# Strassen's seven products for gate and up in the last token block of a bilinear FFN

## The chip, the cores and the metric

The kernel runs on one core of one Trainium2 chip. The metric is the device time of one execution in microseconds (us), the median of the runs shown. A profile is one execution taken by the hardware profiler. The engines are named PE (TensorE, the matmuls), ACT (ScalarE), DVE (VectorE), POOL (GpSimd) and SP (SyncE, which here only issues DMAs); PEld is PE's loading of weights.

## The reference, cut to what matters

S = 2048 tokens, D = 576, 32 query heads of 18 with one key and value head, F = 4608.

```python
x = A_x
h = x + _A_ref(_layernorm(x, axis=-1), A_wq, A_wk, A_wv, A_wo)     # attention
h2 = h + _B_ref(_layernorm(h, axis=-1), B_w_gate, B_w_up, B_w_down)
# _B_ref(x, w_gate, w_up, w_down):
g = jnp.einsum("bsd,df->bsf", x, w_gate)
u = jnp.einsum("bsd,df->bsf", x, w_up)
h = g * u
return jnp.einsum("bsf,fd->bsd", h, w_down)
```

## The kernel before

Tokens go in four blocks of 512 (`NB`, `TB`). Attention runs over pairs of heads and key tiles (`pair`); its work for a block is spread over the FFN of earlier blocks, and it is over in the last third of block 2. After that the FFN has the engines to itself: the end of block 2 and all of block 3, the last.

**Precision.** Matmuls take 32-bit operands rounded for TensorE (F32R). To keep precision each operand is split in a high part (a cast, by ACT or POOL) and a low one (the remainder, by DVE; `split`, lines 92 and 93), and each product takes three matmuls: high x high, high x low, low x high. So each operand costs a cast and a remainder.

**Gate and up** (`ffn`). The FFN has 36 tiles of 128 hidden columns (`NF`) a block. K = 576 is nine chunks of 64 rows. `X` holds the normalised and transposed tokens, split, and the weights of gate stand in the other half of the partitions than those of up: the gate matmul uses array rows 0 to 63 and the up matmul rows 64 to 127 at the same time (line 937), 27 of each of 512 tokens. For this X stands in SBUF twice, with its halves changed about: DMAs "X<-X" copy it. Then ACT copies gate out of PSUM (955), DVE multiplies (959), giving the hidden tile `hf`.

**Down** (`down`). Two hidden tiles make a pair (`NC` = 18 a block). Down is done by Strassen's method over halves of tokens, of hidden columns and of D: `left` makes the sums `S` (834 to 837) and splits them into `A`; the sums of weights come from DRAM ready and split (`wdo`). Fourteen *stages* (`STAGES`) of three matmuls of 288 columns each (line 897, tile y) write three PSUM banks in turn; after each stage DVE adds the bank into the residual `h` (900), or ACT copies it out and POOL adds it (904, 905). A bank is written again three stages later, after it has been read. The last pair of a block (`plain`) uses no Strassen: 48 matmuls.

**Order.** The schedule is written out by hand: instructions run on each engine in the order of the program. Down for a pair runs in one piece behind gate and up of the first tile of the next pair (an even tile), while DVE and ACT prepare the next weights: `load_w` (DMA), `split_w` (POOL casts, DVE takes the remainder). `normal` normalises the tokens of the next block in the last tile of the block before, and `spread` transposes them on PE and splits them into X between the blocks, taking turns with the last down (`both`).

PSUM has eight banks: two tiles of two banks (`ps_s`, in which the last block's gate and up alternate), two of one (`ps_f`), and one each `ps_m` and `ps_a`.

Of the kernel before, what the change touches and what calls it, by code (L numbers as in the profile page):

```python
# [18 lines left out]
F32 = mybir.dt.float32  # L19
# [38 lines left out]
class Block:  # L58


    def __init__(self, tc, x, wq, wkv, wo, wo0, wgu, wd, cst, out):
# [3 lines left out]
        self.wgu, self.wd, self.cst, self.out = wgu, wd, cst, out  # L65
        self.pe, self.act, self.dve, self.sp = tc.nc.tensor, tc.nc.scalar, tc.nc.vector, tc.nc.sync


# [732 lines left out]

    def load_w(self, n):

        if n < NF * NB:
            r = self.wr[n] = self.wp.tile([P, 9, P], F32, tag="wr", bufs=2, name=f"wr{n}")
            self.sp.dma_start(r, self.wgu[n % NF])

    def split_w(self, n):
        if n < NF * NB:
# [33 lines left out]
    def down(self, b, pair):  # L843

        pe, dve, act, sp, pool = self.pe, self.dve, self.act, self.sp, self.nc.gpsimd
        h = self.h[b]
        W = [self.wdo.pop((b, pair, j), None) for j in range(7)]
        if pair == NC - 1:
            ys = {}

            def part(s, n, i):

                ms = [(self.A[:, k, 2 * i + s // 2], W[(1, 0, 2, 3)[2 * i + n]][:, l]) for k, l in ((0, 0), (0, 1), (1, 0))]
                for j, (m, k) in enumerate(ms):
                    pe.matmul(ys[s, n][:, :HD], m[:, s % 2 * P:(s % 2 + 1) * P], k, start=(i == j == 0), stop=(i == 1 and j == 2))  # L855

            if b == NB - 1:
                e = self.ps_s("ye")
                for k, y in enumerate((e[:, 0], e[:, 1], self.ps_f("ye2"), self.ps_f("ye3"), self.ps_m("ye4"), self.ps_a("ye5"))):
                    ys[k // 2, k % 2] = y  # L860
                    part(k // 2, k % 2, 0)
            def add(s, n):
                hs, y = h[:, s, n * HD:(n + 1) * HD], ys.pop((s, n))[:, :HD]
                if b < NB - 1 and n:
                    z = self.tmp[:, self.n_tmp % 5]
                    self.n_tmp += 1
                    act.copy(z, y)
                    pool.tensor_tensor(hs, hs, z, ALU.add)
                else:
                    dve.tensor_tensor(hs, hs, y, ALU.add)  # L870

            for s in range(NQ):
                for n in range(2):
                    if (s, n) not in ys:
                        if b < NB - 1:
                            ys[s, n] = self.ps_y(2 * s + n, f"y{b}_{pair}_{s}_{n}")
                        else:
                            e = self.ps_s("ye6") if n == 0 else e
                            ys[s, n] = e[:, n]
                        part(s, n, 0)  # L880
                    part(s, n, 1)
                    if b < NB - 1:
                        add(s, n)
                        yield
                if b == NB - 1:
                    for n in range(2):
                        add(s, n)
                    yield
                sp.dma_start(self.out[b * TB + s * P: b * TB + (s + 1) * P, :], h[:, s, :])
            return  # L890
        c, a = self.ps_f(f"y{b}_{pair}_2"), self.ps_f(f"y{b}_{pair}_0")
        banks = [a, self.ps_m(f"y{b}_{pair}_1"), c]
        for i, (t, bank, (x, w), first, (s, n), on_dve) in enumerate(STAGES):
            y = banks[bank]
            ms = [(self.A[:, k, x], W[w][:, l]) for k, l in ((0, 0), (0, 1), (1, 0))]
            for j, (m, k) in enumerate(ms):
                pe.matmul(y[:, :HD], m[:, t * P:(t + 1) * P], k, start=(first and j == 0), stop=(j == 2), skip_group_check=True)  # L897
            hs = h[:, t + 2 * s, n * HD:(n + 1) * HD]
            if on_dve:
                dve.tensor_tensor(hs, hs, y[:, :HD], ALU.add)  # L900
            else:
                z = self.tmp[:, self.n_tmp % 5]
                self.n_tmp += 1
                act.copy(z, y[:, :HD])  # L904
                pool.tensor_tensor(hs, hs, z, ALU.add)  # L905
            yield
# [10 lines left out]
    def ffn(self, b):  # L917
        pe, act, dve = self.pe, self.act, self.dve
        X, hid, todo = self.X, [], None
        for f in range(NF):  # L920
            n_ = NF * b + f
            k = f % 2
            w = self.ws.pop(n_)
            on = self.more(b + 2)
            last = f == NF - 1 and b + 1 < NB
            if on:
                pg, pu = self.ps_f(f"pg{n_}"), self.ps_f(f"pu{n_}")
            else:
                gu = self.ps_s(f"gu{n_}")
                pg, pu = gu[:, 0], gu[:, 1]  # L930
            j = 0
            for c in range(9):
                for wk, xk in ((0, 0), (0, 1), (1, 0)):
# [21 lines left out]
            act.copy(g, pg)  # L955
            if on and not last and self.more(b + 2):
# [11 lines left out]
            if f < NF - 1:  # L968
                self.run_aux()
            todo = (f // 2,) if k else None  # L970
        if b + 1 < NB:
            both(self.spread(b + 1), self.down(b, *todo))
            self.load_wd(self.n_wd + 4)
            if b + 2 < NB:
                self.load_x(b + 2)
        else:
            drain(self.down(b, *todo))
# [91 lines left out]
    def run(self):  # L1069
# [12 lines left out]
        with ExitStack() as st:  # L1082
# [79 lines left out]
            del self.oT  # L1162
            self.room()
            self.load_wd(WD_BUFS)
            for b in range(NB):
                self.ffn(b)


# [50 lines left out]
def drain(gen):  # L1219
    for _ in gen:  # L1220
        pass
# [79 lines left out]
```

## Time and profile before

| | |
|---|---|
| median of 3 runs | 2300.15 us (2299.98 to 2305.27) |
| span of the profiled execution, its own time | 2301.0 us |
| PE busy | 2267.3 us, 99% |
| DVE, ACT, POOL busy | 50%, 62%, 28% |
| granted TensorE clock | 0.9 or more of full speed in each of 40 slices |
| last block, from the end of block 2's last gate and up to the end | 1956.0 to 2301.0 us |

The page of the profile gives the span and no other time for that execution. Busy shares are means over parts with different limits: in the first four fifths ACT does the softmax's exponentials, and in the last block it is mostly idle. PE counts as busy while a matmul is in its pipe, so 99% does not mean that it takes a new column in every cycle: the starts of matmuls in the timeline tell that. A row of the chain has start, length and what; a group has busy us, mean ns of one, idle time ahead of it and what ended that; a row of the timeline has start, length, engine, line, operation, tiles and count.

### The profile page before, as it was taken

How to read it: one execution, taken by the hardware profiler on the slowest of the kernel's cores; microseconds unless marked ns; L12 is line 12 of the kernel's file. 1: busy time of each engine (PE TensorE's matmuls, PEld its weight loads, DVE VectorE, ACT ScalarE, POOL GpSimd, SP SyncE). 2: the span in 40 equal slices, each digit the busy share in tenths (PEclk: the TensorE clock that was granted, in tenths of full speed). 3: DMA queues.
4: the chain of work that ended last, by engine and by line, in shares of the span. 5: the costliest groups of instructions: out<-in, count | busy, mean ns of one | idle time of the engine just before them, and what ended most of it. 6: DMA issues, size and time to landing. Idle time of an engine off the chain costs nothing.

```text
span 2301.0 us, 45837 instructions
## 1 busy us (share of the span) xinstructions
PE 2267.3 (99%) x18102; PEld 1605.8 (70%) x18102; DVE 1158.8 (50%) x2047; ACT 1431.8 (62%) x1868; POOL 647.9 (28%) x802
## 2 busy tenths in 40 slices
PE   7999999999999999999999999999999999999999
PEld 5333335777677777777777777776777788888888
DVE  7555635444444445444444445444444476556665
ACT  6889877767776765667776766577776622223322
POOL 5445400222122222222222222212222233333333
PEclk9999999999999999999999999999999999999999
DMA  5778943433344343533343343633343345655553
GB/s 176 232 256 286 300 171 93 123 104 117 116 125 130 119 133 117 189 103 120 112 128 120 118 137 114 191 96 125 124 130 106 123 165 182 202 181 170 171 173 127
DMA packets 158287, 345.38 MB, mean 150 GB/s; under 512 B 16845, under 2 KB 48461, under 8 KB 158069
## 3 DMA queue, kind: packets, MB, share of 16 engines
q1 hardware_dynamic: 155333, 331.16, 44.6%
q0 software_dynamic: 2736, 11.26, 1.6%
q8 instruction: 144, 2.36, 0.4%
q14 instruction: 74, 0.61, 0.1%
HBM read 272.45 MB, written 55.67 MB: 143 GB/s over the span
## 4 chain that ended last, share of the span: by engine, by line
PE 82%; DVE 2%; DMA 2%; ACT 1%; issue 0%; SPq 0%; POOL 0%; DVEq 0%; ACTq 0%
PE pg L937 21%; PE y L897 17%; PE acc L611 15%; PE gu L937 12%; PE s L606 9%; PE pu L937 4%; PE yo L736 3%; PE y L855 1%; DMA q<-q_dram 1%; PE ye L855 0%; DVE ws L93 0%; DMA out_dram<-h 0%; PE tx L785 0%; ACT P L607 0%; DMA X<-X 0%
## 5 line engine op out<-in xcount | busy, mean ns | idle before, releaser
L607 ACT ACTIVATE P<-s 128x1024 f32<-128x1024 f32 x1024 | 1025.5, 1027 | 285.2 <-PE s L606 204.9
L937 PE MATMUL pu<-X,ws 64*128 64x512 f32 x2565 | 693.5, 389 | 0.0
L937 PE MATMUL pg<-X,ws 64*128 64x512 f32 x2565 | 692.8, 389 | 0.0
L905 POOL TENSOR_TENSOR h<-h,tmp 128x288 f32<-128x288 f32 x408 | 317.7, 807 | 916.5 <-ACT tmp L904 915.2
L937 PEld LDWEIGHTS pg<-X,ws 64*128 64x128 f32 x2565 | 475.3, 185 | 67.8 <-DMA wdo<-wd_dram 0.8
L611 PE MATMUL acc<-P,V 128*32 128x512 f32 x4096 | 492.8, 600 | 0.7 <-ACT P L607 0.6
L937 PEld LDWEIGHTS pu<-X,ws 64*128 64x128 f32 x2565 | 472.7, 185 | 10.2
L606 PE MATMUL s<-q,kT 56*128 56x512 f32 x2048 | 439.7, 423 | 6.3 <-ACT P L607 3.8
L897 PEld LDWEIGHTS y<-wdo,room 128*128 128x128 f32 x2856 | 386.1, 188 | 49.7 <-issue 43.3
L897 PE MATMUL y<-wdo,room 128*128 128x288 f32 x2856 | 403.6, 300 | 2.3 <-DVE h L900 2.3
L904 ACT COPY tmp<-y 128x288 f32<-128x288 f32 x408 | 162.6, 399 | 326.4 <-PE y L897 321.9
L900 DVE TENSOR_TENSOR h<-h,y 128x288 f32<-128x288 f32 x544 | 234.6, 453 | 242.0 <-PE y L897 239.2
L606 PEld LDWEIGHTS s<-q,kT 56*128 56x128 f32 x2048 | 197.9, 185 | 207.0 <-ACT P L607 121.1
L937 PE MATMUL gu<-X,ws 64*128 64x512 f32 x2646 | 308.1, 389 | 0.1
L92 POOL CAST ws<-wr 128x1152 fp32r<-128x1152 f32 x144 | 167.7, 1165 | 460.5 <-PE pu L937 293.9
L611 PEld LDWEIGHTS acc<-P,V 128*32 128x32 f32 x4096 | 114.6, 109 | 248.0 <-issue 236.9
L937 PEld LDWEIGHTS gu<-X,ws 64*128 64x128 f32 x2646 | 251.9, 184 | 49.8 <-issue 4.0
L93 DVE TENSOR_TENSOR ws<-wr,ws 128x1152 fp32r<-128x1152 f32 x144 | 197.6, 1372 | 80.7 <-POOL ws L92 80.7
L959 DVE TENSOR_TENSOR hf<-pu,g 128x512 f32<-128x512 f32 x95 | 65.6, 691 | 341.2 <-ACT g L955 341.2
L93 DVE TENSOR_TENSOR room<-S,room 128x1024 fp32r<-128x1024 f32 x68 | 83.3, 1225 | 156.0 <-ACT room L92 156.0
L955 ACT COPY g<-gu 128x512 f32<-128x512 f32 x49 | 28.9, 590 | 134.5 <-PE gu L937 134.5
L92 ACT CAST room<-hf 128x256 fp32r<-128x256 f32 (+1 forms) x144 | 73.9, 513 | 46.6 <-DVE hf L959 46.4
(170 smaller groups left out, 1459.5 us busy)
## 6 DMA issues: line engine op xcount, KB each, us to landing
wdo<-wd_dram SPq DMA_DIRECT2D x492, 288.0 KB
wr<-in_wgu_dram SPq DMA_DIRECT2D x144, 576.0 KB
wd_dram<-wd_room SPq DMA_DIRECT2D x20, 1008.0 KB
q<-q_dram SPq DMA_DIRECT2D x64, 216.0 KB
q_dram<-qs SPq DMA_DIRECT2D x16, 504.0 KB
X<-X SPq DMA_DIRECT2D x28, 256.0 KB
wd_dram<-wd_hi SPq DMA_DIRECT2D x7, 1008.0 KB
wd_dram<-wd_src SPq DMA_DIRECT2D x7, 1008.0 KB
```

What stands on the lines that cost most here:

```text
L92: (copy or self.cast)(hi, src)
L93: self.dve.tensor_tensor(lo, src, f32(hi), ALU.subtract)
L606: self.pe.matmul(s_[:, i], self.kT[o:o + 56, t * P:(t + 1) * P], q[o:o + 56, pr], start=True, stop=True)
L607: self.act.activation(p_, s_, AF.Exp, scale=SCALE)
L611: self.pe.matmul(acc[32 * j:32 * j + 32, :], self.V[:, t, :], Ps[j // 2][:, j % 2, :], start=(t == 0), stop=(t == NT - 1), skip_group_chec ...
L736: pe.matmul(y[:, :HD], m, k, start=(i == 0), stop=(i == len(ms) - 1))
L897: pe.matmul(y[:, :HD], m[:, t * P:(t + 1) * P], k, start=(first and j == 0), stop=(j == 2), skip_group_check=True)
L900: dve.tensor_tensor(hs, hs, y[:, :HD], ALU.add)
L904: act.copy(z, y[:, :HD])
L905: pool.tensor_tensor(hs, hs, z, ALU.add)
L937: pe.matmul(ps, w[o:o + 64, wk, c], X[o:o + 64, xk, c], start=(j == 0), stop=(j == 26))
L959: dve.tensor_tensor(hf, pu, g, ALU.mult)
```

## The change

Block 3 leaves the loop of `ffn`; a new `last_block` does it. For each pair of FFN tiles, gate and up of both tiles are one product of weights and tokens in halves of tokens (256), of K (two halves of 256 rows, the last 64 rows aside) and of F (the two tiles). Strassen's seven products k = 1..7 each take 2 (gate, up) x 2 (chunks of K) x 3 (high and low) matmuls of 128 x 128 weights and 256 tokens, on the whole array. The last 64 rows of K are the *tail*: high and low parts stand in the two halves of the partitions, so it takes 4 x 2 x 2 matmuls a pair. PSUM accumulates products where it can; `c1`, `c5` and `c2` are partial results copied out. Gate is multiplied with up by POOL for three of the four quarters of the hidden pair (`both_halves`) and by DVE for the fourth.

The sums of weights are not stored: `prepare` loads four raw quarters (and the tail), makes three further ones on the way by sums on POOL (raw[7], raw[5], raw[6], raw[3] are its four sums), casts on ACT and takes the remainders on DVE, one step at a time (`do(n)`) between the products of the pair before. The sums of tokens are made in `ahead`, whose steps are called during the last tiles of block 2 (`AHEAD`: tile, then matmul and number of steps; `TURNS`: behind down of that tile). Down's stages for the pair before are dealt between the products (`go`, with `turns` stages a time).

```diff
 # ffn(b), in the loop over f and the 27 matmuls j of gate and up
+            end = b == NB - 2
...
-                    if j == 6 and last:
+                    if j == 6 and last and not end:
                         self.normal(b + 1)
+                    if end and f in AHEAD and j in AHEAD[f]:
+                        for _ in range(AHEAD[f][j]):
+                            next(ahead)
...
             if todo and not on:
                 drain(self.down(b, *todo))
                 self.load_wd(self.n_wd + 7)
+                if end and f in TURNS:
+                    for _ in range(TURNS[f]):
+                        next(ahead)
...
+        if end:
+            self.last_block(ahead, self.down(b, *todo))
+            return
 # new
+    def ahead(self):
+        xh = self.op.tile([P, NQ, 640], F32, tag="ob", name="xhl")
+        for s in range(NQ):
+            dve.tensor_scalar(xh[:, s, 0:D], h[:, s, :], mv[:, s, 0:1], rs[:, s:s + 1], ALU.subtract, ALU.mult)
+            pool.tensor_copy(xh[:, s, D:], xh[:, s, 512:D])
+            if s % 2:
+                yield
...
+        for c in range(5):
+            ps = (self.ps_m if c % 2 else self.ps_a)(f"txl{c}")
+            for s in range(NQ):
+                pe.transpose(ps[:, s * P:(s + 1) * P], xh[:, s, c * P:(c + 1) * P], self.ident)
+            act.copy(raws[c // 2][:, c % 2] if c < 4 else rt, ps)
+            yield
...
+        names = (1, 2, 5, 6, 3, 7, 4)
+        dve.tensor_tensor(low[5], b12, b11, ALU.subtract)
+        dve.tensor_tensor(low[6], b22, low[5], ALU.subtract)
+        yield
+        dve.tensor_tensor(low[4], b21, low[6], ALU.subtract)
+        dve.tensor_tensor(low[7], b22, b12, ALU.subtract)
+        yield
+        for k in names:
+            act.copy(XS[k][:, 0:2], src[k])
+            dve.tensor_tensor(XS[k][:, 2:4], src[k], f32(XS[k][:, 0:2]), ALU.subtract)
+            yield
...
+        prep = self.prepare(0)
+        next(prep)
+        next(prep)
+        yield
...
+        yield from prep
+    def prepare(self, m):
...
+        for i, k in ((0, 1), (3, 5), (2, 4)):
+            sp.dma_start(raw[k], self.wgs[m, :, i])
+        sp.dma_start(self.wt_raw, self.wgt[m])
+        yield
+        sp.dma_start(raw[2], self.wgs[m, :, 1])
+        yield
+        pool.tensor_tensor(raw[7], raw[1], raw[5], ALU.subtract)
+        yield
+        high(0)
+        high(1)
+        yield
+        rest(0)
+        rest(1)
+        pool.tensor_tensor(raw[5], raw[5], raw[4], ALU.add)
+        yield
...
+        rest(6)
+        high(3)
+        yield
+        rest(3)
+        high(7)
+        yield
+        rest(7)
+    def last_block(self, ahead, D):
...
+        def product(k, bank, first=False):
+            W, X = WS[k], self.XS[k]
+            for g in range(2):
+                for c in range(2):
+                    for wk, xk in ((0, 0), (0, 1), (1, 0)):
+                        pe.matmul(bank[:, g * HT:(g + 1) * HT], W[:, wk, c, g], X[:, 2 * xk + c], ...)
...
+        for p in range(NC):
+            a, b_, c = s0[:, p % 2], s1[:, 0], s1[:, 1]
+            turns, loads = ((2, 2, 1, 1, 1, 1), (0, 0, 0, 0, 0, 4)) if p == 0 else ((2, 2, 2, 2, 2, 4), (1, 0, 1, 1, 1, 3))
...
+            product(1, a, True)
+            act.copy(c1, a)
+            do(2)
+            go(0)
+            next(late, None)
+            product(2, c, True)
+            tail(0, 0, c)
+            dve.tensor_tensor(gu11, c, c1, ALU.add)
+            both_halves(a11, gu11)
+            go(1)
+            drain(late)
+            do(1)
+            product(5, b_, True)
+            act.copy(c5, b_)
+            spl(0, a11)
+            go(2)
+            do(2)
+            product(6, a)
+            act.copy(c2, a)
+            go(3)
+            do(3)
+            product(3, b_)
+            tail(0, 1, b_)
+            dve.tensor_tensor(gu12, b_, c2, ALU.add)
+            both_halves(a21, gu12)
+            go(4)
+            do(2)
+            product(7, a)
+            tail(1, 1, a)
+            dve.tensor_tensor(gu22, a, c5, ALU.add)
+            both_halves(a22, gu22)
+            if not plain_:
+                dve.tensor_tensor(S[:, 2], a11, a21, ALU.subtract)
...
+            go(5)
...
+                do(2)
+                dve.tensor_tensor(S[:, 0], a21, a22, ALU.add)
+                dve.tensor_tensor(S[:, 1], S[:, 0], a11, ALU.subtract)
+            product(4, a)
+            tail(1, 2, a)
+            if not plain_:
+                spl(2, a22)
+                spl(3, S[:, 0:3], 3)
+            act.copy(g[:, 0:HT], a[:, 0:HT])
+            dve.tensor_tensor(a12, a[:, HT:], g[:, 0:HT], ALU.mult)
...
+            dve.tensor_tensor(S[:, 3], a12, S[:, 1], ALU.subtract)
+            spl(1, a12)
+            spl(6, S[:, 3])
+            do(1)
+            late = prep
+            D = self.down(b, p)
...
+AHEAD = {28: {8: 1, 14: 1}, 31: {4: 1, 10: 1, 16: 1, 22: 1}, 32: {6: 1, 12: 1, 18: 1, 24: 1}, 33: {12: 1, 18: 1}, 34: {5: 1},
+         35: {1: 1, 3: 1, 6: 1, 8: 1, 11: 1, 13: 1, 15: 1, 18: 1, 21: 1, 24: 1}}
+TURNS = {28: 2, 30: 3}
```

In `last_block`, `spl` casts on ACT and takes the remainder on DVE, `a11`, `a21`, `a12`, `a22` are the quarters of the hidden pair, and for the last pair (`plain_`) down's 48 matmuls stand at the end, 12 of them ahead of product 4. `down` for block 3 loses its own ending, and gives each weight tile free behind its last stage. The host hands over the raw weights in two more layouts, `wgs` and `wgt`.

More of the change, by code (lines that the diff above doesn't have):

```diff
@@ L873, in down @@
                 for n in range(2):
[L874 to L880, printed above, removed]
-                    part(s, n, 1)
[L882 to L887, printed above, removed]
+                    ys[s, n] = self.ps_y(2 * s + n, f"y{b}_{pair}_{s}_{n}")
+                    part(s, n, 0)
+                    part(s, n, 1)
+                    add(s, n)
                     yield
@@ L897, in down @@
                 pe.matmul(y[:, :HD], m[:, t * P:(t + 1) * P], k, start=(first and j == 0), stop=(j == 2), skip_group_check=True)
+            del ms, m, k
+            if all(x[2][1] != w for x in STAGES[i + 1:]):
+                W[w] = None
             hs = h[:, t + 2 * s, n * HD:(n + 1) * HD]
@@ L919, in ffn @@
         X, hid, todo = self.X, [], None
+        ahead = self.ahead()
         for f in range(NF):
@@ L970, in ffn @@
             todo = (f // 2,) if k else None
[L971 to L977, printed above, removed]
+        if end:
+            del X, pg, pu, gu, w, ps, hf, g, self.X
+            self.last_block(ahead, self.down(b, *todo))
+            return
+        both(self.spread(b + 1), self.down(b, *todo))
+        self.load_wd(self.n_wd + 4)
@@ L1164, in run @@
             self.load_wd(WD_BUFS)
-            for b in range(NB):
+            for b in range(NB - 1):
                 self.ffn(b)
```

166 lines of the change are left out of this document (156 added, 10 removed).

## The prediction

> **What bounds the kernel now.** I read the page first, then the chain of waits in order of time over the last token block, the busy time in windows of one pair of FFN tiles, the groups of one shape, and the timeline where the last block starts and ends.
>
> ```profile
> PE 2267.3 (99%) x18102; PEld 1605.8 (70%) x18102; DVE 1158.8 (50%) x2047; ACT 1431.8 (62%) x1868; POOL 647.9 (28%) x802
> 2064.00 12.46 PE gu L937 x108
> 2076.46 5.84 PE y L897 x42
> 2082.30 12.47 PE gu L937 x108
> 1913.00:1931.30 18.30, 18.30 (x153) 15.69 (x152) 11.03 (x20) 5.54 (x12) 6.88 (x9) 1.00 0.52 179
> ```
>
> The first row is the page's; the next three are the chain (start, us, what); the last is a window (PE, PEld, DVE, ACT, POOL busy, granted clock, DMA share, GB/s). In the last block the chain is TensorE alone: 12.47 of gate and up, 5.84 of down, 18.31 us a pair. The clock is full, DVE stands at 11.0 of 18.3, ACT at 5.5, POOL at 6.9. So a saving in matmul time counts in full here until another engine's queue is in the way. (DVE, ACT and POOL queues run in order.)
>
> **TensorE in the new pair.** The old pair is 54 slots of two 64-row matmuls of 512 columns: 12.47/54 = 0.231 us a slot. The new one has 7 x 12 = 84 whole-array matmuls of 256 columns and 16 for the tail of K: 100. No 256-column matmul is in the trace. The nearest:
>
> ```profile
> 2079.72 2.58 PE L897 MATMUL y<-wdo,room 128*128 128x288 f32 x18
> L897 PE MATMUL y<-wdo,room 128*128 128x288 f32 x668 | 93.9, 299 | 0.0
> 46.00 0.40 PE L228 MATMUL psk<-XT,w_l 128*128 128x512 f32 x1
> 46.23 0.39 PE L228 MATMUL psk<-XT,w_h 128*128 128x512 f32 x1
> 1956.09 1.25 PE L785 MATMUL tx<-C,xh 128*128 128x128 f32 x10
> L785 PE MATMUL tx<-C,xh 128*128 128x128 f32 x10 | 1.3, 272 | 0.0
> ```
>
> 288 columns, whole array: (2.58 - 0.30)/17 = 0.134 from start to start. 512 columns, whole array: 0.23, about what two half-array matmuls take together, so one wide matmul is not dearer than one slot. Scaling the nearest row gives 0.119 for 256 columns. Upper bound: 0.134, the 288-column row. Lower bound: the 128-column transposes, (1.25 - 0.27)/9 = 0.109, which looks like the floor for a change of whole-array weights. I take 0.119, from the nearest row: 100 x 0.119 = 11.9 us against 12.47. The Strassen saving of 7.4% in columns (25,600 for 27,648) thus becomes 0.57 us. Down loses its two changes between half and whole array: 5.84 - 42 x 0.134 = 0.21. A pair takes 11.9 + 5.63 = 17.53 if nothing waits, 0.78 less than now.
>
> [...]
>
> **The vector engines.** Rows for the new work (groups of the last block, busy and mean ns; then starts in the timeline):
>
> ```profile
> L900 DVE TENSOR_TENSOR h<-h,y 128x288 f32<-128x288 f32 x128 | 55.5, 454 | 37.9 <-PE y L897 35.7
> L959 DVE TENSOR_TENSOR hf<-gu,g 128x512 f32<-128x512 f32 x30 | 20.6, 687 | 50.7 <-ACT g L955 50.7
> L835 DVE TENSOR_TENSOR S<-S,hf 128x256 f32<-128x256 f32 x15 | 6.4, 426 | 0.5
> L904 ACT COPY tmp<-y 128x288 f32<-128x288 f32 x96 | 38.3, 400 | 82.5 <-PE y L897 82.3
> L92 ACT CAST room<-hf 128x512 fp32r<-128x512 f32 x15 | 9.3, 622 | 11.4 <-DVE hf L959 11.4
> L92 ACT CAST room<-S 128x1024 fp32r<-128x1024 f32 x15 | 15.8, 1055 | 14.5 <-DVE S L837 14.5
> L905 POOL TENSOR_TENSOR h<-h,tmp 128x288 f32<-128x288 f32 x96 | 74.8, 809 | 110.9 <-ACT tmp L904 110.7
> L97 POOL TENSOR_TENSOR wq<-wqr,wq 128x630 fp32r<-128x630 f32 x3 | 4.4, 1463 | 0.2
> 1838.59 0.68 DVE L93 TENSOR_TENSOR room<-hf,room 128x512 fp32r<-128x512 f32 x1
> 1839.19 0.68 DVE L93 TENSOR_TENSOR room<-ob,room 128x512 fp32r<-128x512 f32 x1
> 1839.80 1.22 DVE L93 TENSOR_TENSOR room<-S,room 128x1024 fp32r<-128x1024 f32 x1
> 2090.89 0.42 DVE L836 TENSOR_TENSOR S<-hf 128x256 f32<-128x256 f32 x1
> 2091.23 0.42 DVE L837 TENSOR_TENSOR S<-hf,S 128x256 f32<-128x256 f32 x1
> ```
>
> Back to back, DVE starts a 512-wide one every 0.60 and a 256-wide one every 0.34 (0.46 if it reads the one before); a 768-wide one I put at 0.87, between the 0.60 and a 1024-wide one. DVE per pair: 3 PSUM sums of 512 (1.8), 8 adds into h (8 x 0.41 = 3.3), 4 S sums and one product of 256 (1.7), 4 remainders of 256 and one of 768 (2.2), 8 weight remainders of 512 (4.8): 13.8 us of 17.5, where it was 11. ACT: 3 copies and 8 casts of 512, 6 copies of y, smaller ones: about 12 at the rows' durations. POOL: 6 adds (4.9), 3 products of 256 (2.2), 4 sums of 512, which the rows at 288 and 630 columns put at 1.24 each (5.0): 12. No engine is full; what matters is where the DVE queue is long.
>
> That is at the change of pairs. The last add of the deal before product 4 waits for PE. Behind it in DVE's queue stand, in order: that add 0.41, two weight remainders 1.2, S0 0.34, S1 0.46, then ACT's cast of S (768 wide, between 0.62 and 1.06: 0.85; it covers one small remainder), its remainder 0.87, a12 0.34, S3 0.46, the cast and two small remainders 0.41 + 0.68, the last weight remainder 0.60, and the first add of the next deal 0.41: 7.0, with handovers 7.1 us. The fourth stage of the next deal writes the bank that this add reads. PE gets there after product 4 with tail (16 x 0.119 = 1.90), product 1 (1.43), two stages (0.80), product 2 with tail (1.90) and one stage (0.40): 6.43. So PE waits 0.7 us a pair, from pair 1 on, 17 times: 17.53 + 0.67 = 18.2. Between these points I find no other wait: c1, c5 and c2 are copied a product ahead of their use, product 4 waits for a sum of 0.6 behind 1.6 of stages, A is ready before its stage, and the seven down weights are loaded a pair ahead.
>
> The new weight loads, five of 256 KB a pair, are issued on SP's queue behind product 1, ahead of that pair's down weights, whose landing has a pair's time.
>
> ```profile
> X<-X SPq DMA_DIRECT2D x28, 256.0 KB
> 1959.47 6.35 SPq L797 DMA_DIRECT2D X<-X  x8
> ```
>
> Eight of that size took 6.35 us, 0.8 each; so the two that POOL's first difference needs are there some 4 us after product 1, when POOL comes to it. All of down's POOL adds queue behind it. From the next add on (8.3 us into the pair) POOL has three sums, four adds and two products in one piece, 8.3 us, the last of which is a22 at 16.6; S0's turn in DVE's queue is at about 17.9. So late landings have over a microsecond of slack.
>
> **The two ends.** Around the start of the last block:
>
> ```profile
> 1949.64 6.36 PE gu L937 x54
> 1956.09 0.59 ACT g L955
> 1958.08 0.69 DVE room L93
> 1965.20 6.02 DMA X<-X
> 1997.81 0.69 DVE L959 TENSOR_TENSOR hf<-gu,g 128x512 f32<-128x512 f32 x1 [3.44 <-ACT g L955]
> 1953.50 2.04 DVE L768 TENSOR_SCALAR xh<-h,mvb,yb 128x576 f32<-128x576 f32 x4
> 1889.99 4.71 PE L897 MATMUL y<-wdo,room 128*128 128x288 f32 x33 [1.23 <-DVE h L900]
> 2002.35 1.35 DVE L93 TENSOR_TENSOR ws<-wr,ws 128x1152 fp32r<-128x1152 f32 x1
> 2003.15 5.09 PE L897 MATMUL y<-wdo,room 128*128 128x288 f32 x36
> 2003.84 0.85 DVE L900 TENSOR_TENSOR h<-h,y 128x288 f32<-128x288 f32 x2
> 2289.95 6.88 PE L855 MATMUL ye<-wdo,room 128*128 128x288 f32 x48
> 2296.87 0.82 DVE L870 TENSOR_TENSOR h<-h,ye 128x288 f32<-128x288 f32 x2 [0.90 <-PE ye L855]
> ```
>
> The last gate-and-up of block 2 ends at 1956.0; the span is 2301.0, so 345.0 us are left now. In them the block change waits: for the last hidden tile to be split (to 1958.8) and for X's doubling. In the new kernel product 1 follows at once. Pair 0: 11.9 + 48 x 0.134 = 18.3, and its first stage still waits for the same split, 2.8 us behind the end and some 0.4 of other ACT work, where product 1 and half a stage give 1.8: 1.5 us. So 19.8. Then 17 pairs of 18.2 = 309.4. Behind product 4 of the last pair, down's last 48 matmuls (12 run ahead of it): 6.4. Last matmul to the end of the span stays at 4.2 (2296.8 to 2301.0). Sum: 339.8, or 5.2 less than 345.0.
>
> **The lead-in** moves into block 2 and is not free. (1) The four normalisations go from the last tile, where they were hidden, to tile 28. There down already waits for DVE (the row at 1889.99; DVE runs without a gap before it): 2.0 us. (2) The 20 transposes, which filled a wait at 1956 to 1958, go behind the downs of tiles 28 and 30, with nothing to wait for: 20 x 0.109 = 2.2, plus 0.3 as the fifth waits for its bank. (3) Tile 32 gets four remainders, 2.4 us, into a queue that in such tiles ends (2002.35 + 1.35) 0.55 behind down's start. The first add ends at 2006.5 of that clock instead of 2004.3; the fourth stage, due at 2004.4, waits 2.2. The sums in tiles 31 and 33 fit into DVE's idle time (3.44 us ahead of the product in such a tile), the ten steps in tile 35 into the room that its normalisation and weight split leave. The transposes' copies go ahead of the gate's copy on ACT, which nothing needs at once, as gate and up have two pairs of banks. Sum: 6.7.
>
> Net: -5.2 + 6.7 = +1.5 on a span of 2301.0, which lies 0.85 above the median of the runs (2300.15). Forecast for the median: 2302, no change by 0.3% (6.9 us, about what a measurement of this kernel tells from nothing).
>
> **Rivals.**
> *The queue at the change of pairs is hidden (faster).* For it: 7.1 against 6.43 is a close call, and every DVE price in it is added up without the idle gaps that a queue behind has already used. With no wait: 19.8 + 17 x 17.53 + 10.6 = 328.4, which is 16.6 less, +6.7: 2290. With the floor of 0.109 a matmul instead, PE waits more there (7.1 - 6.0), the pair is 17.6, and the time is 2290 as well; both together (2272) I leave out of the range.
> *The queue is longer (slower).* With the mean durations of the rows (0.45, 0.69, 0.43) in place of their spacing, the same list with its handovers is 8.0 us: POOL is twice as busy as before, and nearly each item waits for ACT, POOL or the item before. PE then waits 1.6 a pair, the pair is 19.1, and the rest 355.1: +10.1 + 6.7, so 2317. It decides from 7.45 us on: 1.0 of wait a pair makes +6.9.
> *The weight loads land late.* Each us beyond POOL's slack comes back at S0. A us in every pair: 2319. Against it: a DMA share of 0.52 now.
> *Whole-array weight loads aren't hidden.* Then each matmul costs 0.109 + 0.119, and the 1,800 products alone add 196 us: 2500. Against it: down's 0.134 includes a change of whole-array weights at every matmul. [...]
>
> **Numbers.** Forecast (2294 to 2308) 0.35; hidden queue 0.32; longer queue 0.29; late loads 0.03; loads not hidden 0.01. Faster: 0.32 and 0.04 of the forecast's edge = 0.36. Slower: 0.29 + 0.03 + 0.01 + 0.04 = 0.37. Same: 0.27. The range takes in the hidden queue or the matmul floor below, with a lead-in that costs some us less than laid out, and the longer queue and late loads above: 2284 to 2322. The forecast's own range is 2294 to 2308.
>
> **What would show it.** Matmuls of the products at 0.119 from start to start; 142 matmuls a pair; the pair 18.2 long, with one wait of PE of some 0.7 us in the fourth stage of the deal, ended by a DVE add into h; no X to X copies, and the wait of 1.5 us in the first deal; down's wait at tile 28 up by 2 us and a new one at tile 32. I am wrong if the products run below 0.112 or above 0.13, if the wait in the fourth stage is absent or above 1 us, or if PE waits for ACT or a load in the middle of a pair.

## The result and the profile after

The changed kernel takes 2438.7 us (median of 4 runs, 2437.5 to 2440.2), the kernel before 2300.2 beside it: a ratio of 1.0596, with the 95% interval 1.0581 to 1.0611. It is slower by 138 us, and the forecast of 2302 us and its range (2284 to 2322) were wrong.

The page of the changed kernel, rows of busy time, of the granted clock in 40 slices, and of the chain by line:

```profile
PE 2304.3 (95%) x17958; PEld 1667.6 (68%) x17958; DVE 1291.1 (53%) x2238; ACT 1528.7 (63%) x2095; POOL 782.7 (32%) x892
...
PEclk9999999999999999999999999999999998888888
...
PE pg L927 19%; PE acc L611 14%; PE y L882 14%; PE s L606 9%; PE pu L927 5%; PE gs L1123 5%; PE yo L736 2%; DVE XW L1064 2%; PE gu L927 1%; ACT room L92 1%; DVE h L888 1%; DVE room L93 1%; DVE wps L1064 1%; DVE S L1215 1%; PE y L855 1%
```

PE issues the 144 matmuls fewer that the change promised and yet is busy 37 us longer, and the clock drops in the last seven slices, which lie in the last block. In the chain, lines of DVE and ACT stand where before there was PE alone. The windows of two neighbouring pairs (length; busy PE, PEld, DVE, ACT, POOL; clock; DMA share; GB/s) and the waits of PE over fifteen pairs (total us, times, longest) say how much of that is waiting. First the windows, then the waits:

```profile
2121.60:2147.20 25.60, 20.49 (x142) 19.80 (x142) 17.62 (x28) 10.54 (x23) 14.66 (x13) 0.90 0.42 128
2147.20:2172.80 25.60, 20.67 (x142) 19.90 (x142) 18.47 (x31) 10.55 (x23) 14.65 (x13) 0.83 0.44 136
```

```profile
PE gs L1123 <- DVE hfl L1234: 51.2, 16, 3.7
PE y L882 <- DVE h L888: 27.8, 15, 1.9
```

A pair is 25.6 us long on the mean (25.1 and 26.1 in turn) where 18.2 was forecast. PE stands idle for 5 us of it: 51.2/16 = 3.2 ahead of a product and 27.8/15 = 1.9 ahead of a stage of down. In the other 20.6 the 142 matmuls are in the pipe, 3 us more than the 17.53 of the prediction. DVE is busy for 18 us instead of 13.8, POOL for 14.7 instead of 12; ACT, at 10.5, is below its 12. The timeline of PE shows both kinds of loss in one pair (start, us, then in brackets the idle time ahead of it and what ended it):

```profile
2136.35 1.58 PE L1123 MATMUL gs<-kT,wss 128*128 128x256 f32 x12
2137.78 0.64 PE L1129 MATMUL gs<-XT_t,wt 128*128 128x256 f32 x4
2138.25 1.35 PE L882 MATMUL y<-wdo,room 128*128 128x288 f32 x9
2141.49 0.66 PE L882 MATMUL y<-wdo,room 128*128 128x288 f32 x3 [1.89 <-DVE h L888]
2141.99 1.58 PE L1123 MATMUL gs<-kT,wss 128*128 128x256 f32 x12
2143.41 0.64 PE L1129 MATMUL gs<-XT_d,wt 128*128 128x256 f32 x4
2147.71 2.93 PE L1123 MATMUL gs<-XS,XW 128*128 128x256 f32 x12 [3.67 <-DVE hfl L1234]
2150.44 1.06 PE L882 MATMUL y<-wdo,room 128*128 128x288 f32 x6
```

At a granted clock of 1.00 (2136.35 to 2137.78) twelve matmuls of a product start within 2137.78 - 2136.35 = 1.43, which is 0.119 each, as forecast. But the last deal stops for 1.89 us, and product 1 of the next pair for 3.67; then product 1 runs at (2150.44 - 2147.71)/12 = 0.23 a matmul, half the pace, at a granted clock of 0.50 over this stretch. What DVE and ACT do meanwhile is in the chain of waits (start, us, what):

```profile
2139.45 0.60 DVE gu L1212
2140.07 0.99 DVE S L1215
2141.07 0.38 DVE h L888
...
2142.19 0.46 DVE h L888
2142.64 2.03 DVE XW L1064 x2
...
2145.04 0.43 DVE S L1226
2145.50 0.84 ACT room L92
2146.36 0.96 DVE room L93
2147.32 0.35 DVE hfl L1234
```

This is the list of the prediction: the last add of the deal, two weight remainders, S0 and S1, the cast of S, its remainder, a12. The prediction had PE run into its end only in the fourth stage of the next deal, 6.4 us after the add that the list begins with. PE stops right behind product 4, until a12 (L1234) is done. Why is the first question. The second is the prices: two remainders take 2.03 where 1.2 was set, and S[:, 2] (L1215), ahead of this list, 0.99 where 0.34 was. The other items of the list are near their prices: from its add to the end of a12 it takes 5.48 (2142.19 to 2147.67) where 4.47 was set. The groups of the fifteen pairs (busy us, mean ns) sort the prices:

```profile
L1064 DVE TENSOR_TENSOR XW<-raw,XW 128x512 fp32r<-128x512 f32 x56 | 59.4, 1083 | 0.2
...
L1215 DVE TENSOR_TENSOR S<-hfl 128x256 f32<-128x256 f32 x15 | 14.9, 996 | 0.4
...
L888 DVE TENSOR_TENSOR h<-h,y 128x288 f32<-128x288 f32 x120 | 52.1, 448 | 33.8 <-PE y L882 33.1
...
L1206 DVE TENSOR_TENSOR cs<-gs,cs 128x512 f32<-128x512 f32 x15 | 10.2, 678 | 0.0
...
L893 POOL TENSOR_TENSOR h<-h,tmp 128x288 f32<-128x288 f32 x90 | 92.5, 1035 | 3.5 <-ACT tmp L892 3.5
...
L1087 POOL TENSOR_TENSOR raw<-raw 128x512 f32<-128x512 f32 x15 | 26.1, 1741 | 0.0
```

DVE's operations with one operand in PSUM (L888, L1206) cost what they did before, 0.45 and 0.68. Many of those with both operands in SBUF are dearer: 1.08 for 512 columns, where 0.68 was measured before, and 1.0 for 256 (L1215), where it was 0.43. But not all: S0 and S1 (L1225, L1226) still take 0.41 and 0.43. POOL's are dearer too: its adds take 1.04 instead of 0.81, and two of its four sums of 512 take 1.74, the others 1.29 and 1.46, where I had 1.24.

**Ledger.** By the profiled spans, 2435.7 against the 2302.5 that the prediction's sum stands for: +133.2. Product 1 of pair 0 starts at 1963.3, near the forecast 1962.7, but only because the blocks before it ran 3.9 us shorter in this execution (tile 27's gate and up begins at 1870.6 instead of 1874.5). Pair 0 takes 29.3 instead of 19.8, the other 17 pairs 432.6 (25.45 each) instead of 309.4, the end 10.45 instead of 10.6: +9.5, +123.2 and -0.1. So the question is a pair. Counted in another way: from product 1 of pair 0 to the end the changed kernel takes 472.4 us, where the kernel before has 345.0 left behind the last gate and up of block 2. These 127.4 and the lead-in, 11.8 when measured alone (e5 below), make 139 of the 138.5 by which the medians differ.

### The profile page after: what moved, and what is told of

Same layout as the page of the kernel before. It is cut to its first block, busy times and chain, and to the rows that moved or that the text cites. A ratio compares the mean times of both kernels' runs of the same rounds, so it can differ in the third digit from the quotient of the medians.

```text
span 2435.7 us, 46083 instructions
## 1 busy us (share of the span) xinstructions
PE 2304.3 (95%) x17958; PEld 1667.6 (68%) x17958; DVE 1291.1 (53%) x2238; ACT 1528.7 (63%) x2095; POOL 782.7 (32%) x892
## 4 chain that ended last, share of the span: by engine, by line
PE 71%; DVE 10%; ACT 3%; issue 3%; POOL 1%; DMA 1%; SPq 0%; DVEq 0%; ACTq 0%; POOLq 0%
PE pg L927 19%; PE acc L611 14%; PE y L882 14%; PE s L606 9%; PE pu L927 5%; PE gs L1123 5%; PE yo L736 2%; DVE XW L1064 2%; PE gu L927 1%; ACT room L92 1%; DVE h L888 1%; DVE room L93 1%; DVE wps L1064 1%; DVE S L1215 1%; PE y L855 1%
## 5 line engine op out<-in xcount | busy, mean ns | idle before, releaser
L893 POOL TENSOR_TENSOR h<-h,tmp 128x288 f32<-128x288 f32 x408 | 342.5, 863 | 802.5 <-ACT tmp L892 801.7
L882 PE MATMUL y<-wdo,room 128*128 128x288 f32 x2856 | 429.3, 304 | 38.2 <-DVE h L888 38.2
L882 PEld LDWEIGHTS y<-wdo,room 128*128 128x128 f32 x2856 | 399.3, 193 | 84.1 <-DVE h L888 43.3
L888 DVE TENSOR_TENSOR h<-h,y 128x288 f32<-128x288 f32 x544 | 235.1, 451 | 243.0 <-PE y L882 241.9
L92 POOL CAST ws<-wr 128x1152 fp32r<-128x1152 f32 x108 | 126.6, 1173 | 382.2 <-PE pu L927 224.8
L93 DVE TENSOR_TENSOR ws<-wr,ws 128x1152 fp32r<-128x1152 f32 x108 | 148.9, 1379 | 60.8 <-POOL ws L92 60.8
L93 DVE TENSOR_TENSOR room<-S,room 128x1024 fp32r<-128x1024 f32 (+1 forms) x85 | 86.1, 1012 | 157.3 <-ACT room L92 156.8
L1123 PE MATMUL gs<-XS,XW 128*128 128x256 f32 x540 | 84.5, 313 | 33.6 <-DVE hfl L1234 33.2
L1123 PEld LDWEIGHTS gs<-XS,XW 128*128 128x128 f32 x540 | 77.9, 216 | 37.7 <-DVE hfl L1234 35.1
L92 ACT CAST room<-S 128x1024 fp32r<-128x1024 f32 (+1 forms) x85 | 74.0, 871 | 37.4 <-DVE S L1226 30.9
L1132 POOL TENSOR_TENSOR hfl<-gu 128x256 f32<-128x256 f32 x36 | 26.9, 747 | 185.8 <-DVE gu L1190 184.7
```

Source lines behind the costliest of these rows:

```text
L92: (copy or self.cast)(hi, src)
L93: self.dve.tensor_tensor(lo, src, f32(hi), ALU.subtract)
L1123: pe.matmul(bank[:, g * HT:(g + 1) * HT], W[:, wk, c, g], X[:, 2 * xk + c], start=(first and g == c == wk == xk == 0), stop=(c == 1 and wk ...
```

## The experiments

Two causes were on the table. **By tile:** a product that writes one bank waits for the reader of the other bank of the same tile, here 3.2 us on the mean. The two `a` banks are halves of the tile s0, so product 1 of pair p + 1 waits for a12 of pair p, which reads the other half. The prediction had taken banks as separate. **POOL beside DVE:** the two lengthen each other where both take their operands from SBUF (in the rows above 1.08 for 0.68 on DVE and 1.04 for 0.81 on POOL), and that moves DVE's list at every point. The rivals of that were a simple lack of DVE time, and plain mis-pricing of the 512-wide remainders.

**e1_banks** takes the a banks from two tiles.

```
-        s0, s1 = self.ps_s("gs0"), self.ps_s("gs1")
+        s0, s1, sb = self.ps_s("gs0"), self.ps_s("gs1"), self.ps_a("gsb")
...
-            a, b_, c = s0[:, p % 2], s1[:, 0], s1[:, 1]
+            a, b_, c = (s0, s1)[p % 2][:, 0], sb[:, :], (s0, s1)[p % 2][:, 1]
```

> The products' PSUM banks are given to three tiles so that no two products that wait on different readers share a tile. Theory 1 (a wait is kept by the PSUM tile, not by the bank, so product 1 waits for DVE's read of the other half of the tile): the wait of 3 to 4 us ahead of product 1 goes, product 1 falls from 2.9 to about 1.45 us as the clock stays up, PE then waits 1 to 2 us in the fourth stage of the deal and still 2 us in the last deal; a pair falls from 25.6 to 21 to 22.5 us, the time from 2438 to 2365 to 2390. Rival (product 1 truly needs what DVE makes there): the wait stays, 2430 to 2445.

Measured: 2402.2 us (2401.5 to 2402.9), ratio 1.0439 (1.0419 to 1.0460), a pair of 23.2 us: 36.5 us better than the changed kernel, but a miss upward. PE's waits in the last block:

```profile
PE gs L1123 <- ACT cs L1184: 32.9, 16, 2.8
PE y L882 <- DVE h L888: 29.8, 15, 2.1
```

The wait of product 1 for a12, 16 times and 3.2 us on the mean in the changed kernel, is gone with nothing changed but which tile a bank belongs to, which shows the first cause. In its place stands one of the same kind that I had made myself: a and c now share a tile, so product 2 (into c) waits for ACT's copy c1 out of a.

**e2_nosums** leaves POOL's four weight sums out (products 3, 6 and 7 then use other weights) and keeps the banks of the changed kernel.

```
+        raw = {**raw, 7: raw[4], 6: raw[1], 3: raw[2]}
...
-        pool.tensor_tensor(raw[7], raw[1], raw[5], ALU.subtract)     (and the three others)
```

> The changed kernel without POOL's four sums of weights a pair (products 3, 6 and 7 then use other weights, so part of the computation is left out). Theory 2 (DVE's instructions with two SBUF inputs and POOL's instructions hold each other up): DVE's weight remainders (512 wide) fall from a mean of 1.1 to about 0.7 us, POOL's adds into h from 1.03 to 0.8, PE's wait in the last deal shrinks below 0.5 and the one ahead of product 1 by about 1 us: a pair of 21.5 to 23, 2375 to 2400. Rival (DVE's queue is long by count alone): remainders stay at 1.0 or more, 2425 to 2440.

Measured: 2381.8 us, ratio 1.0351 (1.0330 to 1.0372), a pair of 22.45. A group and the waits:

```profile
L1065 DVE TENSOR_TENSOR XW<-raw,XW 128x512 fp32r<-128x512 f32 x49 | 40.4, 848 | 0.2
```

```profile
PE gs L1120 <- DVE hfl L1231: 39.8, 14, 2.8
PE y L882 <- DVE h L888: 5.3, 14, 0.6
```

The same remainders on DVE fall from 1.08 to 0.85 with nothing changed but what POOL does, and the wait in the last deal from 1.9 to 0.6 at most. The time and the pair are as expected, but three points are not: the remainders were expected at 0.7, POOL's adds into h stay at 1.02 instead of falling to 0.8, and the wait ahead of product 1 falls only from 3.2 to 2.8, not by 1 us.

**e3_both** is e1 and e2 together.

> Both edits. If the two causes are all there is beside the prediction's own steps, a pair comes to 18 to 18.8 us (the prediction's 18.2) and the time to 2303 to 2318, with the granted clock at 0.98 or more and one wait of PE under 1 us a pair in the fourth stage. If DVE's queue is too long by count, the pair stays above 19.5 and the time above 2330.

Measured: 2349.4 us, ratio 1.0210 (1.0189 to 1.0230), most pairs 20.4. Here I missed by 31 us, for the reason that e1's own waits show: product 2 waits for c1.

```profile
PE gs L1120 <- ACT cs L1181: 29.6, 15, 2.0
```

The layout of e1 and e3 was therefore no clean test of what is left when all tile waits are gone; e6 and e9 are.

**e4_pool** asks for the second cause alone, without any of the change: the kernel before, with two products of 512 columns on POOL in each tile of the last block, which nobody reads.

```
+                    if j == 4 and b == NB - 1:
+                        for _ in range(2):
+                            self.nc.gpsimd.tensor_tensor(scr[:, 0], scr[:, 0], scr[:, 1], ALU.mult)
```

> The kernel before with two further POOL products of 512 columns (SBUF in and out, result unused) in each tile of the last block, queued right behind the weight cast. Theory 2: DVE's sums S (256 wide, 0.42 to 0.43 us) and weight remainders (1.35) in the last block become longer where they meet POOL, S to 0.6 or more on the mean, POOL's own 512-wide ones take over 1.3, and DVE's products and adds that read PSUM (0.69, 0.45) stay; the time goes up by 0 to 20 us as the odd tile has 0.7 us to spare. Rival (no contention): all DVE means within 3% of before and the time within 0.2%.

Measured: 2329.3 us (2326.5 to 2336.2), ratio 1.0129 (1.0108 to 1.0150). Work of POOL that nothing waits for costs this kernel 28.6 us, more than the 0 to 20 expected. PE's waits over fourteen pairs, groups of its last block, and four lines of its timeline:

```profile
PE y L897 <- DVE h L900: 17.3, 14, 1.2
```

```profile
L835 DVE TENSOR_TENSOR S<-S,hf 128x256 f32<-128x256 f32 x14 | 19.6, 1400 | 0.5
...
L900 DVE TENSOR_TENSOR h<-h,y 128x288 f32<-128x288 f32 x112 | 48.1, 453 | 31.7 <-PE y L897 31.7
...
L965 DVE TENSOR_TENSOR hf<-gu,g 128x512 f32<-128x512 f32 x28 | 19.3, 688 | 18.0 <-ACT g L961 18.0
```

```profile
2117.97 2.72 POOL L947 TENSOR_TENSOR scr<-scr 128x512 f32<-128x512 f32 x2
2118.23 1.31 DVE L834 TENSOR_TENSOR S<-hf,hf 128x256 f32<-128x256 f32 x1
2119.57 1.40 DVE L835 TENSOR_TENSOR S<-S,hf 128x256 f32<-128x256 f32 x1
2120.90 0.41 DVE L836 TENSOR_TENSOR S<-hf 128x256 f32<-128x256 f32 x1
```

L834 and L835 start inside POOL's two products and take 1.31 and 1.40, close to the 1.36 of one such product; L836 starts after POOL has ended and takes 0.41, as before. L835 was 0.426 in the kernel before. The operations with an operand in PSUM (L900, L965) don't notice: 0.45 and 0.69, as before. So in these rows a DVE instruction of 0.43 with both operands in SBUF lasts as long as the POOL instruction beside it. DVE's adds into h come later by that, and PE waits for one of them in every pair, 1.2 us.

**e6_banks2** is a layout in which no product has to wait for a late reader of a sibling bank: a and b_ swap sides between two tiles, c has one of its own.

```
+            a, b_, c = (s0, s1)[p % 2][:, 0], (s1, s0)[p % 2][:, 1], sb[:, :]
```

> The products' banks again, now so that product 2 shares its tile with nothing and product 5 with the pair before's product 4 (in e1_banks product 2 waited up to 3.1 us for ACT's copy of product 1, as both were in one tile). Theory 1 with a queue of DVE that contention has made long: the wait ahead of product 2 goes, and PE waits 1.5 to 2.5 us in the fourth stage instead, so a pair of 21.5 to 22.8 and 2370 to 2400. Rival (the shared tile was all that held it): a pair below 21, under 2365.

Measured: 2373.7 us, ratio 1.0315 (1.0292 to 1.0337), a pair of 21.8, as expected. One releaser is left (waits over fifteen pairs), and a group of the weight remainders:

```profile
PE y L882 <- DVE h L888: 40.8, 22, 2.1
```

```profile
L1064 DVE TENSOR_TENSOR XW<-raw,XW 128x512 fp32r<-128x512 f32 x48 | 50.8, 1080 | 0.2
```

By PE's timeline the wait of 2.1 is in the last deal of every pair; the wait of the fourth stage, up to 1.4, is there in only some of them, where it had been expected in all. The tile waits are worth 25.6 - 21.8 = 3.8 us a pair, 65 us in all (2438.7 - 2373.7). The remainders are as dear as in the changed kernel, 1.08: this layout leaves POOL's work as it was.

**e7_adds** is e6 with all adds into h of the last block on DVE, straight from PSUM, so that POOL loses six adds a pair and DVE gains them.

> e6_banks2 with down's adds into h in the last block all on DVE (which reads y from PSUM), none on ACT and POOL. Theory 2 (what counts is POOL's time against DVE's instructions with two SBUF inputs): POOL falls from 13 to 8 us a pair, the weight remainders to 0.7 to 0.9 us, and although DVE gets 2.5 us more work, a pair falls to 20 to 21.5: 2345 to 2380. Rival (DVE's count of work decides): a pair grows by 1 to 2.5 us over e6_banks2.

Measured: 2349.6 us, ratio 1.0210 (1.0186 to 1.0233), a pair of 20.2, as expected; remainders 0.78, DVE busy for 88.8 of 100 us. ACT's six copies of y go too. DVE with three quarters more adds is quicker than DVE beside POOL. That speaks against a mere lack of DVE time.

**e8_noprep** is e6 with the weights prepared for pairs 0 and 1 only: all casts, remainders, sums and loads of weights are gone from pair 1 on.

```
-            prep = self.prepare(p + 1) if p + 1 < NC else iter(())
+            prep = self.prepare(p + 1) if p == 0 else iter(())
```

> e6_banks2 with the weights prepared for pairs 0 and 1 alone and used again by the others (loads, sums, casts and remainders of the other pairs are left out). What is left is TensorE and the handling of the hidden tiles: a pair of 17.5 to 18.0 us by the prediction's 0.119 and 0.134 and no wait over 0.3 us; 2292 to 2306, as the lead-in and pair 0 keep their cost. If whole-array matmuls or the order of the products cost more than laid out, the pair stays above 18.5 and the time above 2315.

Measured: 2315.4 us, ratio 1.0073 (1.0050 to 1.0096). The pair is 18.08, just above what I expected; the total was expected below 2306 and lies just above the 2315 that was set for dearer matmuls. PE's waits over 15 pairs, and a stretch of 100 us:

```profile
PE y L882 <- DVE h L888: 4.4, 15, 0.3
```

```profile
2200.00:2300.00 100.00, 98.52 (x790) 97.34 (x790) 54.38 (x117) 36.24 (x85) 37.26 (x49) 1.00 0.38 111
```

Here the granted clock is 1.00 and PE is busy for 98.5 of 100 us. POOL's adds into h, with no sums and remainders beside them, are back at 0.81. The pair of TensorE is thus what the prediction said: 18.08 less the wait, 0.3 idle and 0.5 from start to start, is 17.6, against 17.53. So the matmuls are not dearer. Yet with its weights for nothing the change still loses 15 us: pair 0, in which the preparation still runs, takes 25.1 us and pair 1 20.1, while the other pairs win 0.23 each on the 18.31 of before. From product 1 to the end it takes 346.7 us, against the 345.0 of the kernel before, and the lead-in comes on top.

**e9_nosums2** is e6 without POOL's sums, that is, both causes treated.

> e6_banks2 (no product waits through a shared PSUM tile) without POOL's four sums of weights (that part is left out; products 3, 6 and 7 use other weights). With theories 1 and 2 as the two causes, what stays is the prediction's own pair: 18.2 to 19.0 us, with a wait of 0.6 to 1.3 in the fourth stage and 0.3 in the last deal, as POOL's adds into h still meet the weight remainders (0.85 us each in e2_nosums, not 0.6): 2308 to 2326. Rival (a third cause): a pair of 19.5 or more, over 2335.

Measured: 2324.4 us, ratio 1.0094 (1.0066 to 1.0123), most pairs 18.97, 19.1 on the mean, at the upper end of what was expected. PE's waits over some 14 pairs, then the group of weight remainders:

```profile
PE y L882 <- DVE h L888: 15.4, 29, 1.2
```

```profile
L1065 DVE TENSOR_TENSOR XW<-raw,XW 128x512 fp32r<-128x512 f32 x51 | 41.8, 841 | 0.2
```

There are now two waits a pair, 0.53 on the mean: by PE's timeline one of 0.35 in the last deal and one of 0.59 in the fourth stage, the one that the prediction had placed there at 0.67. Pair 0 takes 19.4.

**e10_quiet** adds the edit of e7 to e9.

> e9_nosums2 with down's adds into h on DVE as well, so that POOL has three products a pair left. If contention with POOL's adds is what still lengthens DVE's queue, the weight remainders fall to 0.69 us, and the pair stays within 0.5 us of e9_nosums2 although DVE has 2.5 us more work. If DVE's count decides by now, the pair is 1 to 2 us longer than in e9_nosums2.

Measured: 2329.1 us, ratio 1.0115 (1.0087 to 1.0143), most pairs 19.05, within 0.5 us of e9 as expected. The same group:

```profile
L1065 DVE TENSOR_TENSOR XW<-raw,XW 128x512 fp32r<-128x512 f32 x51 | 34.1, 691 | 0.2
```

With hardly any POOL work beside them (busy for 31 of 271 us) the remainders are back at 0.69, the price of the kernel before. So their size was not mis-read; POOL made the difference, all of it. The pair gains nothing; DVE has six more adds in it, and that this is the reason was not tested.

**e5_leadin** is the kernel before with the lead-in alone (normalisations, transposes, sums and splits in tiles 28 to 33, their result unused; block 3 as before). **e11_half** is that without the sums and splits of tiles 31 to 33.

> The kernel before with the lead-in alone: the last block's tokens are normalised, transposed, summed and split in the tiles of block 2 as in the change, and the result isn't used. The prediction's 6.7 us: 2305 to 2310, with down's wait at tile 28 up by 2 us, a new one of about 2 at tile 32 and 2.5 for the transposes. Rival (the changed kernel's 7.3 us came from the weights' preparation in tile 35 as well): below 2304.

> e5_leadin (plus 11.8 us) without the sums and splits of tokens in tiles 31 to 33: the normalisations in tile 28 and the transposes behind down of tiles 28 and 30 are left. The prediction's share of these is 4.5 us; by the trace of the changed kernel, where down of tile 28 ends 4.6 us and of tile 30 1.8 us later than before, it is 6 to 7: 2305 to 2308.

Measured: e5 2311.9 us, ratio 1.0044 (1.0026 to 1.0062), so +11.8; e11 2308.2, ratio 1.0029 (1.0018 to 1.0040), so +6.6. e5 is just above what was expected, e11 at the upper edge. The chain of e5 around tiles 28, 31 and 32:

```profile
1891.40 1.96 DVE xhl L994 x4
1893.77 6.17 PE y L897 x33
...
1927.15 2.15 DVE XS L1028 x2
...
1935.11 2.40 DVE XS L1028 x3
```

In tile 28 down waits for the four normalisations, as forecast: 3.19 instead of 1.23, so 1.96 longer. But then its 33 matmuls take 6.17, where the prediction's row of the kernel before has 4.71: the first thirteen start 0.24 us or more apart instead of 0.13, at a granted clock of 0.73 over this piece. In tile 31 two remainders that should have gone into idle time take 1.07 each, beside POOL's cast of weights (in the changed kernel's trace 2.23 for both, beside a cast of 1.16), and end too late; in tile 32 three more stand ahead of down, which waits for 3.50 and then runs slowly in the same way (6.00 for its 33 matmuls). In the changed kernel the time from the end of one tile's gate and up to the next tile's start grows from 7.5 to 12.1 in tile 28, from 5.7 to 7.5 in tile 30 and from 5.8 to 10.7 in tile 32: 11.3 us in sum. In e5 and e11 it grows by the same amounts, within 0.2, in the tiles where they have this work.

No run beat the kernel before, and none points to a version that would: e8, which pays nothing for the weights after pair 1, is the fastest with the new block and still slower. The two causes of the pair, with the other one in and out: separate tiles are worth 65 us with POOL's sums in (changed kernel to e6) and 57 with them out (e2 to e9); leaving the sums out is worth 57 us with the shared tile (changed kernel to e2) and 49 without it (e6 to e9). Together they are 114 of the 138.5. What is left in e9, 24 us, is the lead-in, 11.8, and a last block that is 12.8 longer (357.8 from product 1 to the end, for 345.0).

## Why the prediction was wrong, step by step

**Right.** The matmul of 256 columns at 0.119 and with it the pair of TensorE at 17.53 (e8: 17.6 without waits). The weight loads, whole-array and hidden: in e8's 100 us PE loads weights 790 times for its 790 matmuls, and the pair is still at 17.6, so the rival of 2500 us is out. The end at 10.6 (10.45). The place of the wait in the fourth stage: in e9 it stands there at 0.59. But this is the kernel with both causes removed; in the changed kernel PE never meets the queue there.

**Wrong: "Between these points I find no other wait".** Product 1 waits for a12 each time, 3.2 us a pair on average. The step says why c1, c5 and c2 make nobody wait and names no wait for product 1, as if the two a banks were free of each other. The dependency goes by tile, as e1 shows (no wait for a12 where the two a banks are in two tiles), and s0 holds both. The DVE list in front of a12 was laid out rightly item by item; only the point where PE meets it was put a whole product, two stages and more too late. By e6 this is 65 us of the 138, with the part of the slower clock that hangs on it (granted 0.87 from 2019 to 2300 in the changed kernel, 0.95 in e6). The sentence fails in a second place: PE also waits 1.9 us in the last deal, for an add into h that stands in DVE's queue behind S[:, 2]. This wait stays when the tiles are separate (e6) and falls to 0.4 without POOL's sums (e2), so it belongs to the next point.

**Wrong: the prices of DVE's list.** Both rivals at this place took their prices from the rows of a kernel whose POOL had half the work. The slower one named the right suspect ("POOL is twice as busy as before") but priced it at 0.43 and 0.69 an item, the means of before; beside POOL S[:, 2] and the weight remainders take 1.0 and 1.08. A sum of the prediction's own terms points at it, with what e4 showed afterwards. The operations of DVE with two operands in SBUF are S sums 1.4, small remainders 2.2 and weight remainders 4.8, together 8.4. POOL's work was 12. If these went one at a time, as the times of L834 and L835 beside POOL's products in e4 suggest (1.31 and 1.40 beside 1.36), they would need 20.4 us in a pair of 17.5, an estimate from these numbers. e6, the layout without tile waits, has a pair of 21.8; e9, with POOL at 7, needs 15.4 and has 19.1. That this sum is the bound in itself no run has shown, since the order in DVE's queue plays into it. What is shown: the four sums cost 2373.7 - 2324.4 = 49 us when the tile waits are out, and all of the preparation 58 (2373.7 - 2315.4, e8).

**Not foreseen: the clock.** The prediction counts a wait at its own length and has no term for slower matmuls behind it. But behind the wait of 3.67 PE runs at half pace, at a granted clock of 0.50; product 1 alone then takes 1.3 us longer. Over whole pairs the granted clock is 0.90 and 0.83 in the two windows above. Shorter waits are followed by slow matmuls too, in some pairs: behind one of 2.06 in e6 the next twelve matmuls take 2.67 instead of 1.58 (rows in the last section). How long a wait has to be for that no run has shown. The starts of the matmuls in PE's timeline divide a pair, on the mean of pairs 2 to 16. In the changed kernel it is 17.5 of matmuls at their full pace, 5.9 of stops at the waits (idle time and restart) and 2.3 that the matmuls at the slower pace add; in e6 17.5, 3.1 and 1.2; in e9 17.5, 1.4 and 0.2; in e8 17.5, 0.5 and 0.1. So the slow matmuls go when the waits go, and I count them as an effect of the waits.

**Mis-sized: the lead-in.** 6.7 forecast, 11.8 measured alone (e5). The normalisations and transposes were set at 4.5 and measured at 6.6, the sums and splits at 2.2 and measured at 5.2 (11.8 - 6.6). For the second one reason is seen in tile 31: "fit into DVE's idle time" overlooked POOL's cast (1.07 for a remainder beside it, where 0.60 was set), and down of tile 32 waits for 3.50 instead of 2.2. The rest is again the clock (in the changed kernel granted at 0.73 over down of tile 28 behind its wait, and at 0.76 over that of tile 32): in tile 28 the wait grows by the 2.0 forecast, and the slow start of down behind it costs another 1.4; in tile 32 it costs 1.2.

**Mis-sized: pair 0**, 29.3 for 19.8. "Its first stage still waits for the same split" was right; but by PE's timeline that wait is 3.25, not 1.5:

```profile
1968.67 0.53 PE L855 MATMUL y<-wdo,room 128*128 128x288 f32 x2 [3.25 <-ACT room L92]
```

The product of the split tile stands in DVE's queue behind weight remainders of up to 1.78 us, beside POOL's sums. Two more waits in the pair's further course, 1.0 ahead of product 4 and 4.0 ahead of the next product 1, make up most of the rest. The runs divide it as they do the later pairs: with separate tiles pair 0 takes 25.1 (e6), and without POOL's sums as well 19.4 (e9), near the forecast.

## What to carry to other kernels

Before a new buffer layout is priced, list for every bank the tile that it belongs to, and let each writer wait for the last reader of any part of that tile: here two banks that alternate in one tile cost 3.8 us a pair against separate ones (e6). When work goes to POOL because it is idle, add its time to DVE's operations with two operands in SBUF, stage by stage, and look at whether the sum fits; here a weight remainder of 512 columns takes 1.08 in pairs with POOL busy for 14.7 of 25.6 us, and 0.69 where it was busy for 31 of 271 (e10). Where a change adds waits to PE, add a term for the matmuls behind them (1.3 us behind the wait of 3.67, 1.4 behind one of 3.19). And a saving of 0.8 us in 18 on the bounding engine is smaller than the error of a queue estimate of seven items, so the preparation that it needs has to be priced first.

## What the runs showed that was not expected

Two POOL products a tile which nothing depends on cost 28.6 us (e4): a DVE instruction of 0.43 takes 1.31 to 1.40 beside one of 1.36 on POOL, and one that reads PSUM stays at 0.45 and 0.69. The changed kernel pays twice for a wait: after 3.67 idle PE does the next twelve matmuls in 2.73 instead of 1.43, at a granted clock of 0.50 instead of 1.00. And a wait of 2 us is sometimes followed by such a slow product and sometimes not; in e6 the same wait in two pairs in a row, by PE's timeline:

```profile
2119.22 1.09 PE L882 MATMUL y<-wdo,room 128*128 128x288 f32 x3 [2.06 <-DVE h L888]
2120.10 2.67 PE L1123 MATMUL gs<-kT,wss 128*128 128x256 f32 x12
...
2141.07 0.66 PE L882 MATMUL y<-wdo,room 128*128 128x288 f32 x3 [2.06 <-DVE h L888]
2141.57 1.58 PE L1123 MATMUL gs<-kT,XW 128*128 128x256 f32 x12
```
